# Block 0's transposes and the first two experts' sums of squares on TensorE, a routing step without GpSimd, and a new order of events

## The chip, the cores and the metric

One Trainium2 chip; the program runs on one of its cores. The metric is device time in microseconds (us) of one execution, lower is better. TensorE is PE in the rows, VectorE DVE, ScalarE ACT, GpSimd POOL; SP is the engine that issues the DMAs.

## The reference, cut to what matters

```python
x = attn(q, k, v, n_global=8, n_local=96)      # (2, 8, 768, 64): each row sees 8 global and 96 local keys
x = x.transpose(0, 2, 1, 3).reshape(1536, 512)
# MoE 1: dense, 4 experts
out = 0
for e in range(4):
    out += p[:, e:e + 1] * (np.maximum(x @ w1[e], 0) @ w2[e])     # w1[e] 512x1024, w2[e] 1024x512
x = out
# MoE 2: greedy, 8 experts with 192 places each
logits = x @ w_gate                            # (1536, 8)
# go through all (token, expert) pairs by falling logit; a pair is taken if its token
# has no expert yet and its expert has a free place
for e in range(8):
    mask = assigned == e
    out[mask] = np.maximum(x[mask] @ v1[e], 0) @ v2[e]
```

## The kernel before

All products run in fp16. A float32 operand is scaled by a power of two and split into a high and a low fp16 part (`hi`, `lo`), and three products of the parts are added. The power of two comes from a sum of squares: for a weight matrix ("job" k; jobs 0 to 7 are w1, w2 of the four experts of MoE 1, jobs 8 to 23 those of MoE 2) each half of 128x2048 is loaded by `w_load` (L397, 1 MB, issued on SP), squared on ACT with a running sum (`w_norm`, L437), the two sums go through a product with a matrix of ones (L441), `pow2` makes the scale on DVE (L316 to L321), and `w_split` makes the high parts on ACT (L548) and the low parts on DVE (L462), four pieces of 128x1024 each. A half's buffer is free for the next load when its second low part is done.

**First stage (to about 400 us).** Attention over 12 blocks of 128 tokens, interleaved with the products of experts 0 and 1 of MoE 1. Events of a block carry its number behind a dot (none for block 0): `load`, `loadv`; `sq0` to `sq2` (squares of v, k, q), `total`, `scale`; `hi0`, `lo0` and so on; `T0`, `T1` (transposes of q and k), `swap` (the two halves of q's heads exchanged); `qk0` to `qk3` (scores, L686 to L693), `max`, `exp` (L705, L707), `ph`, `pl` (high and low parts of the probabilities), `PT0`, `PT1` (their transposes), `pv` (L744), `x`, `norm`, `xhi`, `xlo`, `xT` (transpose of the attention's result). `g`, `relu`, `hhi`, `hlo`, `y` are the products of expert 0 (first product L825), `G`, `Relu`, `Hhi`, `Hlo`, `Y` those of expert 1; `wl`, `wsq`, `wsum`, `wsc`, `whi`, `wlo` prepare the weights. The transposes are DMAs (L633, L729, L761), and so are the two halves of `swap` (L626, L627). The order of the events is written out by hand in ORDER1, with the engine behind a slash where it isn't the usual one; every engine works its own part of it in that order.

**Second stage (to about 633 us).** Experts 2 and 3, the logits and their ranks; the events are sorted by times in a table (TIMES3). `pump` carries the preparation of the next weights on by one step.

**Routing (L1106 to L1199).** Seven iterations, each a chain on DVE with four short trips to PE: `best` (M, m, D), `pick` (a product and a sum, L1128 and L1130), `below` (v L1136, twelve products on PE L1141, a count L1144), `spread` (a product L1150), `pick`, `below`, `spread`, and the new `cut`. Behind each trip `between` puts some of the 93 deferred second products of expert 3 on PE (`fill`, L1003: two 512-column products each), steps of the finished token blocks (`side_step`: `add` L1013, `norm` L1019, and `rows_steps`, which scales a block, splits it into `hi` and `lo` and writes it to DRAM as rows, L1045 to L1058), and `pump`, as the list HOPS says.

**Last stage.** `gather` (L1207, on POOL's queue) fetches the rows of each expert of MoE 2 by the routing's indices, `gather_T` transposes them (L1216, on SP), and eight experts follow (first products L1238, second L1258). It can't start before the last block of rows has been written.

Of the kernel before, what the change touches and what calls it, by code (L numbers as in the profile page):

```python
# [45 lines left out]

ORDER1 = """
    load gate0 sq1 sq0 loadv wl0 gate1 slope4 gate2 sq2 total wl1 scale slope2 hi1 hi0/V lo0 diag/A slope3 wl0.1 wsq0
    load.1 wsq1 slope0 wsum wsq0.1 slope1 T0 lo1 wl1.1 T1 tiles.1 sq1.1 swap wsc slope5 whi1/G whi0/V wlo1 whi3 whi2
    wlo3 hi2/G lo2 qk0 sq0.1 wlo2 loadv.1 slope6 wlo0 wsq1.1 load.2 max0 sq2.1 wsum.1 wl0.2 wsc.1 qk1 whi1.1/G exp0  # L50
    total.1 slope7 scale.1 max1 hi1.1 hi0.1/V qk2 exp1 max2 qk3 lo0.1 exp2 whi2.1/G lo1.1 ph0/G wl1.2 T0.1 both
    whi3.1/V wsq0.2 sq1.2 pl0/G probs loadv.2 T1.1 wsq1.2 max3 ph2 wsum.2 whi0.1/V swap.1 ph1/G wlo1.1 exp3 pl1 sq0.2
    wlo0.1 diag.1/A wlo2.1 keys.1 ph3 wlo3.1 wsc.2 kglob.1 wl0.3 hi2.1 sq2.2 pl2/G qk0.1 total.2 pl3/G max0.1 wl1.3
    exp0.1 scale.2 qk1.1 PT0 hi1.2 tiles hi0.2/G max1.1 whi2.2/G lo0.2 exp1.1 qk2.1 ph0.1/G PT1 wsq0.3 lo2.1 qk3.1
    T0.2 max2.1 lo1.2 load.3 T1.2 consts diag.2 swap.2 pv keys.2 max3.1 x wsq1.3 norm ph1.1/A kglob.2 loadv.3 sq1.3
    values.1 exp2.1 pl0.1/G wsum.3 qk0.2 rscale xhi/G wsc.3 xlo exp3.1 xT pl1.1 vglob.1 gate3 ph2.1/A pl2.1 max0.2
    sq0.3 sq2.3 qk1.2 hi2.2/G total.3 g00 g01 scale.3 ph3.1/G hi1.3/V pe max1.2 exp0.2 pl3.1/G whi1.3 g02 hi0.3 g03
    lo1.3 qk2.2 whi0.2/G PT0.1 lo0.3 ph0.2 PT1.1 lo2.2 T0.3 g10 g11 pv.1 hi2.3 whi1.2 Both wlo2.2 g12 relu0 g13 max2.2
    exp1.2 T1.3 hhi0 x.1 pl0.2/G qk3.2 hlo0 norm.1 rscale.1 xhi.1/V y0 relu1 hhi1 exp2.2 load.4 xlo.1 max3.2 keys.3 y1
    sq1.4 y2 swap.3 exp3.2 hlo1 ph2.2/A ph1.2/G y3 y4 xT.1 diag.3 y5 kglob.3 pl1.2/G loadv.4 wlo1.2 y6 qk0.3 wlo0.2  # L60
    whi3.2 qk1.3 PT0.2 sq0.4 g00.1 max0.3 g01.1 g02.1 lo2.3 sq2.4 ph3.2 total.4 exp0.3 whi0.3 g03.1 pl2.2/G g10.1
    scale.4 qk2.3 max1.3 relu0.1/V y7 values.2/A g11.1 hi1.4/V g12.1 g13.1 pl3.2/G G00 lo1.4 G01 diag.4 max2.3 load.5
    ph0.3 vglob.2 exp1.3 hi0.4/G sq1.5 G02 relu1.1 hhi1.1 exp2.3 qk3.3 wlo3.2 PT1.2 ph1.3 hhi0.1 lo0.4 sq0.5 T1.4 pe.1
    ph2.3/A max3.3 loadv.5 G03 hlo0.1 hlo1.1 pv.2 exp3.3 y0.1 T0.4 G10 pl0.3 Tiles G11 y1.1 x.2 ph3.3 norm.2 pl1.3/G
    pl2.3/G sq2.5 pl3.3/G PT0.3 values.3/G swap.4 y2.1 y3.1 rscale.2 y4.1 keys.4/A y5.1 y6.1 whi3.3 whi2.3 total.5
    xhi.2/V kglob.4 hi2.4 PT1.3 Relu0 xlo.2 scale.5 Hhi0 qk0.4 qk1.4 hi1.5/G G12 G13 vglob.3 max0.4 hi0.5/G Relu1
    max1.4 pv.3 wlo3.3 x.3 y7.1 lo2.4 xT.2 Hhi1 g00.2 wlo0.3 norm.3 g01.2 load.6 g02.2 Hlo0/G g03.2 lo1.5 tiles.2
    exp0.4 g10.2 rscale.3 g11.2 Hlo1/G xhi.3/V xlo.3 qk2.4 g12.2 wlo1.3 sq1.6 loadv.6 relu0.2 exp1.4 max2.4 sq0.6
    lo0.5 add qk3.4 xT.3 g13.2 G00.1 wlo2.3 Pe hhi0.2 T0.5 Y0 G01.1 T1.5 sq2.6 total.6 hi2.5/V hlo0.2 Y1 ph0.4/G lo2.5
    pl0.4/G pe.2 scale.6 diag.5/A ph1.4/A add.1/V hi1.6/G Y2 Y3 relu1.2/V exp2.4 pl1.4/G hi0.6/V keys.5/G Y4 G02.1 Y5  # L70
    load.7 G03.1 Y6 ph2.4/A max3.4 exp3.4 Y7 kglob.5 sq1.7 pl2.4 y0.2 lo1.6 y1.2 swap.5 qk0.5 y2.2 sq0.7 ph3.4/A G10.1
    hhi1.2/V Tiles.1 PT0.4 y3.2 Relu0.1 pl3.4 G11.1 G12.1 hlo1.2/G max0.5 G13.1 g00.3 qk1.5 diag.6 hi2.6/V exp0.5 Pe.1
    qk2.5 loadv.7 g01.3 ph0.5/G y4.2 Hhi0.1 values.4/G lo0.6 sq2.7 max1.5 PT1.4 total.7 g02.3 Relu1.1/V Hhi1.1/G
    max2.5 g03.3 Hlo0.1 exp1.5 T1.6 qk3.5 exp2.5 vglob.4 scale.7 y5.2 pl0.5/G Hlo1.1 T0.6 y6.2 y7.2 pv.4 ph1.5/G Add
    Y0.1 hi1.7/V g10.3 max3.5 g11.3 swap.6 exp3.5 tiles.3 pl1.5 qk0.6 ph2.5/G hi0.7/V qk1.6 Y1.1 values.5 g12.3
    vglob.5 x.4 g13.3 max0.6 lo2.6 relu0.3 lo1.7 Y2.1 pl2.5 load.8 sq1.8 G00.2 hhi0.3 Y3.1 exp0.6 qk2.6 T1.7 max1.6
    lo0.7 hlo0.3/G loadv.8 Y4.1 G01.2 PT0.5 hi2.7/V relu1.3/V exp1.6 max2.6 norm.4 qk3.6 hhi1.3/V sq0.8 ph3.5/G T0.7
    rscale.4 sq2.8 G02.2 Y5.1 G03.2 hlo1.3/G pl3.5 PT1.5 diag.7/A max3.6 Y6.1 keys.7/A add.2/V xhi.4/V Relu0.2 total.8
    pe.3 G10.2 xlo.4 scale.8 lo2.7 hi1.8/V Y7.1 G11.2 exp2.6 Tiles.2 y0.3 hi0.8 y1.3 y2.3 y3.3 ph0.6/G y4.3 G12.2 y5.3
    pl0.6/G ph2.6/G Hhi0.2/V exp3.6 y6.3 lo1.8 pv.5 hi2.8/G xT.4 load.9 Add.1 Hlo0.2/G ph1.6/G swap.7 G13.2 loadv.9  # L80
    ph3.6/A lo2.8 x.5 pl2.6 pl1.6 Pe.2 Relu1.2 sq1.9 sq0.9 g00.4 sq2.9 y7.3 kglob.7 g01.4 qk0.7 g02.4 g03.4 total.9
# [1730 lines left out]
```

## Time and profile before

| | |
|---|---|
| time, median of 3 runs | 886.25 us (885.26 to 886.25) |
| profiled execution, its own time | 888.71 us |
| span of the profile | 886.9 us |
| mean granted TensorE clock | 0.971 |
| busy: PE, DVE, ACT, POOL | 775.8, 618.0, 500.4, 250.1 us |

The profiled execution lies 2.5 us above the median, and 1.8 us of it lie outside the span.

### The profile page before, as it was taken

The page shows a single profiled execution, that of the slowest core. Times are in us where ns is not written, and L with a number is a line of the kernel's source. Part 1 is how long each engine was busy: PE and PEld are TensorE (multiplying, and loading weights), DVE is VectorE, ACT ScalarE, POOL GpSimd, SP SyncE. Part 2 cuts the span into 40 slices and gives each one's busy share as a digit, 9 for nine tenths or more (in the row PEclk, how much of TensorE's full clock was granted, in tenths as well). Part 3 has the DMA queues.
Part 4 walks back from the last instruction along what each step waited for, and adds up shares of the span by engine and source line. Part 5 has one row for each costly group of instructions (what it writes and reads, how often), then busy time and mean ns, then how long its engine had stood idle before and what let it go on. Part 6 is the DMA issues. An engine that isn't in the chain of part 4 may idle for free. (4 is left out here: it accounts for less than half of the span.)

```text
span 886.9 us, 20995 instructions
## 1 busy us (share of the span) xinstructions
PE 775.8 (87%) x8540; PEld 594.9 (67%) x8545; DVE 618.0 (70%) x1557; ACT 500.4 (56%) x978; POOL 250.1 (28%) x299
## 2 busy tenths in 40 slices
...
GB/s 238 273 201 167 135 161 158 143 149 101 81 71 181 49 49 49 160 127 26 13 14 24 2 26 24 26 96 2 167 72 72 73 233 320 225 256 337 177 37 38
DMA packets 196865, 105.31 MB, mean 119 GB/s; under 512 B 167584, under 2 KB 167584, under 8 KB 196768
## 3 DMA queue, kind: packets, MB, share of 16 engines
...
q0 software_dynamic: 2048, 6.34, 3.0%
...
## 5 line engine op out<-in xcount | busy, mean ns | idle before, releaser
L825 PEld LDWEIGHTS <-w 128*128 128x128 f16 x3456 | 246.4, 98 | 31.2 <-issue 0.6
L825 PE MATMUL pH<-xT,w 128*128 128x128 f16 (+1 forms) x3168 | 246.9, 234 | 0.4 <-ACT H L799 0.4
L836 PE MATMUL pY<-w,hh 128*128 128x512 f16 x544 | 161.8, 379 | 0.0
L836 PE MATMUL pY<-w,hl 128*128 128x512 f16 x272 | 103.1, 379 | 1.6 <-DVE hl L1385 1.6
L971 ACT ACTIVATE Cj<-C 128x128 bf16<-128x128 bf16 (+11 forms) x88 | 75.3, 855 | 42.4 <-DVE C L958 41.5
L1238 PEld LDWEIGHTS <-w 128*128 128x128 f16 x768 | 67.4, 102 | 23.0 <-DMA xg<-g 17.2
L799 ACT ACTIVATE H<-pH 128x512 f32<-128x512 f32 (+1 forms) x83 | 46.1, 561 | 60.0 <-PE pH L825 48.5
L958 DVE TENSOR_SCALAR C<-w,Lg 128x1024 bf16<-128x1024 f32 (+7 forms) x112 | 72.6, 665 | 3.8 <-PE pw L977 1.8
L836 PEld LDWEIGHTS <-hh 128*128 128x128 f16 x544 | 47.3, 98 | 34.5
L1238 PE MATMUL pH<-xg,w 128*128 128x192 f16 x528 | 51.7, 258 | 17.8 <-DMA xg<-g 16.7
L1258 PE MATMUL pR<-hh,w 128*128 128x192 f16 x512 | 67.0, 249 | 0.0
L1258 PEld LDWEIGHTS <-w 128*128 128x128 f16 x768 | 65.3, 100 | 0.3
L1258 PE MATMUL pR<-hl,w 128*128 128x192 f16 x256 | 63.9, 250 | 0.0
L1003 PE MATMUL pY<-w,xT 128*128 128x512 f16 x192 | 62.4, 400 | 0.0
L707 ACT ACTIVATE t<-pS,mx,ec 128x256 f32<-128x256 f32 (+1 forms) x96 | 51.6, 541 | 2.7 <-issue 0.4
L550 POOL TENSOR_SCALAR hh<-H 128x512 f16<-128x512 f32 x38 | 26.4, 696 | 89.2 <-ACT H L799 57.6
L836 PEld LDWEIGHTS <-hl 128*128 128x128 f16 x272 | 26.6, 98 | 34.9 <-DVE hl L1385 3.3
L722 POOL TENSOR_TENSOR pp<-t,pp 128x512 f16<-128x512 f32 (+1 forms) x27 | 35.3, 1306 | 41.1 <-DVE pp L552 20.6
L462 DVE SCALAR_TENSOR_TENSOR w<-raw,wsr,w 128x1024 f16<-128x1024 f32 x32 | 40.3, 1278 | 9.0 <-ACT w L548 8.8
L1003 PE MATMUL pY<-w,hl 128*128 128x512 f16 x112 | 45.5, 406 | 0.0
L552 DVE TENSOR_SCALAR hh<-H 128x384 f16<-128x384 f32 (+1 forms) x48 | 18.7, 389 | 38.3 <-ACT H L799 38.2
L961 DVE SCALAR_TENSOR_TENSOR jk<-w,Lg,notbefore 128x128 bf16<-128x128 f32 x96 | 42.6, 444 | 0.0
...
## 6 DMA issues: line engine op xcount, KB each, us to landing
w<-in_moe_w_dram SPq DMA_DIRECT2D x16, 1024.0 KB, 7.0
raw<-in_moe_w_dram SPq DMA_DIRECT2D x16, 1024.0 KB, 7.9
hl<-in_moe_w_dram SPq DMA_DIRECT2D x8, 1024.0 KB, 5.5
y<-in_moe_w_dram SPq DMA_DIRECT2D x4, 1024.0 KB, 8.0
xT<-in_moe_w_dram SPq DMA_DIRECT2D x4, 1024.0 KB, 8.1
rows<-xs SPq DMA_DIRECT2D x12, 260.0 KB, 2.0
...
```

The source lines that it names most:

```text
L462: V.scalar_tensor_tensor(l, r[:, d2], sc, h, op0=OP.mult, op1=OP.subtract)
L707: s.nc.scalar.activation(t[:, hh], ps[:, hh], AF.Exp, bias=mx[:, 1, hh:hh + 1], scale=e[:, 0:1], accum_out=s.SU[j][:, 2 * g + hh:2 * g + h ...
L722: (G if eng == "G" else V).tensor_sub(pl[:, x], t, ph[:, x])
L799: s.nc.scalar.activation(H, ps, AF.Relu, scale=HS)
L825: nc.tensor.matmul(o[f], w[:, d, 128 * (f0 + f):128 * (f0 + f) + 128], x[:, :, c], start=(d == 0 and i == 0), stop=(d == 3 and i == 2))
L836: nc.tensor.matmul(py, l[:, f], w[:, f], start=(f == 0 and i == 0), stop=(f == 7 and i == 2))
L958: V.tensor_scalar(C[:, 8 * i:8 * i + n], x[:, :n, e], l, None, op0=OP.is_ge)
L961: V.scalar_tensor_tensor(jk, s.LRof[j][:, e], l, s.notbefore, op0=OP.is_equal, op1=OP.mult, accum_out=s.AC[j][:, 0, e:e + 1])
L971: s.nc.scalar.activation(x, C, AF.Copy, accum_out=s.AC[j][:, 1, e:e + 1])
L1003: nc.tensor.matmul(py, a[:, f], w[:, f], start=(n == 0), stop=(n == 23))
L1238: nc.tensor.matmul(ps[0][:, f % 2], w[:, d, 128 * f:128 * f + 128], xg[:, :, c], start=(k == 0), stop=(k == 11))
L1258: nc.tensor.matmul(ps[0][:, d % 2], w[:, f, 128 * d:128 * d + 128], h[:, f], start=(k == 0), stop=(k == 23))
```

## The change

1. **Block 0's transposes.** With TURNED = 1 the `T0`, `T1`, `swap`, `PT0`, `PT1` and `xT` of block 0 are products with an fp16 identity matrix on TensorE (`turn`), four at a time into a PSUM tile that ACT or DVE copies out. The other blocks keep their DMA transposes.
2. **Squares by TensorE.** With BYPE = 4 the sums of squares of jobs 0 to 3 are 32 products each of the weights' upper bf16 halves with themselves, whose diagonal DVE adds up.
3. **Sums in bf16.** The sums of squares are held in bf16, so the product with ones is a bf16 one.
4. **ORDER1** is written anew, with some events on other engines.
5. **Second stage:** pumps become events of the same table; the list ORDER3 is empty, so events are sorted by the same times.
6. **`rows_steps`** is now one ACT operation for `hi`, a DVE one for `lo`, and a small ACT operation for the scale; POOL keeps a memset.
7. **`route`** takes the rank from the minimum by two shifts, instead of a `pick`.
8. **`between`** calls `pump` once each, and the weights' preparation stops ahead of the splits of jobs 8 and 9 until the 29th call (`s.limit`).

```diff
     def w_norm(s, k, q):
+        if k < BYPE and q < 2:
+            if q == 0:
+                J["gram"] = s.pY.tile([128, 512], F32, name="pY")[:, 0:128]
+            x = s.raws[k, q][0].bitcast(BF)
+            for a in range(4):
+                for b in range(4):
+                    y = x[:, a, 256 * b + 1:256 * b + 256:2]
+                    nc.tensor.matmul(J["gram"], y, y, start=(q + a + b == 0), stop=(q == 1 and a + b == 6))
+            return
+        if k < BYPE and q == 2:
+            jk = s.sm.tile([128, 128], BF, name="gramj", bufs=1)
+            V.scalar_tensor_tensor(jk, J.pop("gram"), 1.0, s.ident, op0=OP.mult, op1=OP.mult, accum_out=J["ss"][:, 0:1])
+            J["ps"] = s.pw[:, k:k + 1]
+            nc.tensor.matmul(J["ps"], s.ones, J["ss"][:, 0:1], start=False, stop=True, skip_group_check=True)
+            return
...
+    def turn(s, o, parts):
+        nc = s.nc
+        for a in range(0, o.shape[1], 4):
+            ps = s.pH.tile([128, 4, 128], F32, name="pH")
+            for i in range(4):
+                n = 0
+                for x in parts(a + i):
+                    m = x.shape[1]
+                    nc.tensor.matmul(ps[n:n + m, i], x, s.identh, start=True, stop=True)
+                    n += m
+            if a % 8:
+                nc.vector.tensor_copy(o[:, a:a + 4], ps)
+            else:
+                nc.scalar.activation(o[:, a:a + 4], ps, AF.Copy)
...
     def rows_steps(s, j, sc, inv):
-            if late:
-                s.scaled_on("V" if j == s.NB - 1 else "A", xs[:, 0:512], x, sc)
-            else:
-                nc.scalar.activation(x, x, AF.Copy, scale=sc)
-                nc.scalar.copy(xs[:, 0:512], x)
-            nc.gpsimd.tensor_scalar(xs[:, 1024:1026].bitcast(F32), inv, 1.0 / HS, 0.0, op0=OP.mult, op1=OP.add)
+            s.scaled_on("V" if j == s.NB - 1 else "A", xs[:, 0:512], x, sc)
+            nc.scalar.activation(xs[:, 1024:1026].bitcast(F32), inv, AF.Copy, scale=1.0 / HS)
             nc.gpsimd.memset(xs[:, 1026:], 0.0)
...
-            if late:
-                nc.vector.scalar_tensor_tensor(xs[:, 512:1024], x, sc, xs[:, 0:512], op0=OP.mult, op1=OP.subtract)
-            else:
-                nc.gpsimd.tensor_sub(xs[:, 512:1024], x, xs[:, 0:512])
+            nc.vector.scalar_tensor_tensor(xs[:, 512:1024], x, sc, xs[:, 0:512], op0=OP.mult, op1=OP.subtract)
...
         for it in range(E - 1):
-            D = best()
-            r = pick(D, s.R, "r")
+            D, m = best()
+
+            r = rk.tile([128, NB], I32, name="r")
+            V.tensor_scalar(r, m, 21, 21, op0=OP.logical_shift_left, op1=OP.logical_shift_right)
...
-            s.loadlimit, s.limit = 16, 10
+            s.loadlimit, s.limit = 16, 8
...
             def between():
-                fill(HOPS[2 * s.nfill])
+                fill(HOPS[s.nfill])
                 s.nfill += 1
...
-                s.pump(HOPS[2 * s.nfill - 1])
+                s.pump(1)
+                if s.nfill > 28:
+
+                    s.limit = 10
+                    s.pump(3)
```

On SP's queue at the start of the program, before (the transposes are L633 of block 0, the swap is L626 and L627; y and xT hold the halves of job 0 and 1, and xT again of job 2):

```order
5 L475 DMA y<-in_moe_w_dram 128x4x512 x2
6 L475 DMA xT<-in_moe_w_dram 128x4x512
7 L560 DMA x<-in_k_dram 128x8x64
8 L560 DMA x<-in_q_dram 128x8x64
9 L633 DMA_TRANSPOSE qT<-qn 128x8x128
10 L475 DMA xT<-in_moe_w_dram 128x4x512
11 L633 DMA_TRANSPOSE kT<-kn 128x8x128
12 L626 DMA qT<-qT 64x1024
13 L627 DMA qT<-qT 64x1024
```

The same place of the changed kernel:

```order
5 L494 DMA y<-in_moe_w_dram 128x4x512 x2
6 L494 DMA xT<-in_moe_w_dram 128x4x512 x2
7 L579 DMA x<-in_k_dram 128x8x64
8 L579 DMA x<-in_q_dram 128x8x64
9 L579 DMA x<-in_v_dram 128x8x64
10 L579 DMA x<-in_k_dram 128x8x64
11 L579 DMA x<-in_q_dram 128x8x64
12 L494 DMA y<-in_moe_w_dram 128x4x512 x2
13 L675 DMA_TRANSPOSE qT<-qn 128x8x128
```

Block 0's four DMAs are gone from between the loads; block 1's q transpose is the first one left.

On DVE in the second iteration of the routing, before (L1128 and L1130 with R are the `pick` of the rank, L462 a low part of job 8):

```order
1092 L1120 TENSOR_REDUCE m<-M 128x12
1093 L1122 TENSOR_TENSOR D<-M,m 128x96
1094 L1128 TENSOR_TENSOR pt<-D,R 128x96
1095 L1130 TENSOR_REDUCE r<-pt 128x12
1096 L1136 TENSOR_TENSOR v<-r,t_9917 128x480
1097 L462 SCALAR_TENSOR_TENSOR w<-w_9913,wsr,w 128x2x512
1098 L1144 TENSOR_SCALAR vt,kk<-pq 8x40
1099 L1013 SCALAR_TENSOR_TENSOR y<-pY,pe_5_6348,y 128x512
```

The corresponding piece of the changed kernel, in its fifth iteration:

```order
1111 L1158 TENSOR_REDUCE m<-M 128x12
1112 L1160 TENSOR_TENSOR D<-M,m 128x96
1113 L1195 TENSOR_SCALAR r<-m 128x12
1114 L1174 TENSOR_TENSOR v<-r,t_10115 128x480
1115 L1182 TENSOR_SCALAR vt,kk<-pq 8x40
1116 L1059 SCALAR_TENSOR_TENSOR y<-pY,pe_8_6553,y 128x512
```

One shift stands for two operations, and no low part of the weights lies between v and its count.

On ACT behind the routing, before (sqj is `norm` of block 10 and 11, xs the `hi` of block 10; the splits of raw and w_9913 are job 10's; junk is the square of a later job):

```order
407 L1019 ACTIVATE sqj,rq_10731<-y 128x512
408 L548 ACTIVATE w<-w_9914,wsr 128x1024
409 L548 ACTIVATE xs<-y,rgr 128x512
410 L1019 ACTIVATE sqj,rq_10775<-y 128x512
411 L548 ACTIVATE w_10812<-raw,wsr 128x2x512 x2
412 L548 ACTIVATE w_10812<-w_9913,wsr 128x2x512 x2
413 L437 ACTIVATE junk,wss<-raw 128x2048
```

The same place of the changed kernel (row 415 writes the scale of block 11 into its rows, w_10111 is the buffer that held job 8's halves and is loaded again with the second half of job 10 for row 413 and the first of job 11 for row 417; w_10112 is job 9's):

```order
407 L1065 ACTIVATE sqj,rq_10871<-y 128x512
408 L456 ACTIVATE y,wss<-raw 128x2048
409 L567 ACTIVATE w<-w_10111,wsr 128x2x512 x2
410 L567 ACTIVATE xs<-y,rgr 128x512
411 L1088 ACTIVATE xs<-rgr 128x1
412 L1065 ACTIVATE sqj,rq_10923<-y 128x512
413 L456 ACTIVATE y,wss<-w_10111 128x2048
414 L567 ACTIVATE w<-w_10111,wsr 128x2x512
415 L1088 ACTIVATE xs<-rgr 128x1
416 L567 ACTIVATE w<-w_10112,wsr 128x1024 x2
417 L456 ACTIVATE y,wss<-w_10111 128x2048
```

Squares of jobs 10 and 11 and the last high part of job 8 now stand ahead of row 415, which belongs to the last block of rows.

On DVE at the same place of the changed kernel (rows 1177 and 1179 are `hi` and `lo` of block 11, rows 1168, 1178 and 1180 low parts of jobs 8 and 9):

```order
1167 L1059 SCALAR_TENSOR_TENSOR y<-pY,pe_11_6559,y 128x512
1168 L481 SCALAR_TENSOR_TENSOR w<-w_10111,wsr,w 128x2x512
1169 L1093 SCALAR_TENSOR_TENSOR xs<-y,rgr,xs 128x512
...
1177 L571 TENSOR_SCALAR xs<-y,rgr 128x512
1178 L481 SCALAR_TENSOR_TENSOR w<-w_10111,wsr,w 128x2x512
1179 L1093 SCALAR_TENSOR_TENSOR xs<-y,rgr,xs 128x512
1180 L481 SCALAR_TENSOR_TENSOR w<-w_10112,wsr,w 128x1024 x3
```

The last low part of job 8 stands between `hi` and `lo` of block 11; before, the two were neighbours.

On SP around the last rows, of the changed kernel (before, both loads of w_9913 stood ahead of the last six row writes):

```order
151 L400 DMA raw<-in_moe_w_dram 128x4x512
152 L1096 DMA rows<-xs 128x1040 x9
153 L400 DMA w_10111<-in_moe_w_dram 128x4x512
154 L1096 DMA rows<-xs 128x1040 x2
155 L400 DMA w_10111<-in_moe_w_dram 128x4x512
156 L1096 DMA rows<-xs 128x1040
157 L1256 DMA_TRANSPOSE xg<-g 128x8x96 x4
```

The second of those loads now stands directly ahead of the write of block 11.

## Rows read from the trace of the kernel before

**Rows 1.** Busy time by stretch, windows view: length, each engine's busy us, granted clock, DMA share.

```profile
core 0: us, PE busy (x) PEld busy (x) DVE busy (x) ACT busy (x) POOL busy (x), PEclk, DMA share, GB/s
...
30.00:40.00 10.00, 2.65 (x16) 1.89 (x13) 9.96 (x20) 8.54 (x22) 4.73 (x7) 1.00 0.96 258
...
100.00:150.00 50.00, 48.13 (x644) 37.27 (x643) 44.82 (x101) 32.89 (x95) 21.77 (x20) 1.00 0.75 137
...
633.00:700.00 67.00, 56.99 (x385) 25.07 (x383) 53.63 (x164) 35.77 (x52) 14.17 (x27) 0.90 0.28 99
```

**Rows 2.** PE's timeline, first 64 us: start, duration, operation, idle before and what ended it.

```profile
26.01 0.27 PE L692 MATMUL pS<-kT,qT 128*128 128x128 f16 x1 [6.61 <-DMA kT<-kn]
...
42.53 0.31 PE L692 MATMUL pS<-kT,qT 128*128 128x128 f16 x1
42.63 0.31 PE L693 MATMUL pS<-kT,qT 128*128 128x128 f16 x1
...
52.40 1.70 PE L744 MATMUL pO<-vs,pt 128*128 128x64 f16 x24 [3.40 <-DMA pt<-pp]
...
63.09 1.07 PE L825 MATMUL pH<-xT,w 128*128 128x128 f16 x10
```

**Rows 3.** ACT's groups by line in the first 64 us: busy, mean ns of one, idle before.

```profile
L437 ACT ACTIVATE w<-y 128x2048 f16<-128x2048 f32 x4 | 7.6, 1906 | 2.3 <-DMA y<-in_moe_w_dram 2.3
```

**Rows 4.** DMA issues in the first 64 us: KB each, median us from issue to landing.

```profile
pt<-pp SPq DMA_TRANSPOSE x4, 3.9
...
kT<-kn SPq DMA_TRANSPOSE x3, 4.3
```

**Rows 5.** DVE's timeline in the routing: end of iteration 5, iteration 6, and a disturbed v.

```profile
674.42 0.14 DVE L1168 TENSOR_TENSOR cut<-cut,pq 128x8 f32<-128x8 f32 x1
...
675.77 0.26 DVE L1128 TENSOR_TENSOR pt<-D,R 128x96 f32<-128x96 bf16 x1
...
676.35 0.66 DVE L1136 TENSOR_TENSOR v<-r,t 128x480 bf16<-128x480 f32 x1
...
682.19 0.16 DVE L1168 TENSOR_TENSOR cut<-cut,pq 128x8 f32<-128x8 f32 x1 [0.31 <-PE pq L1150]
...
688.36 1.62 DVE L1136 TENSOR_TENSOR v<-r,k 128x480 bf16<-128x480 f32 x1
```

**Rows 6.** POOL's timeline beside that v.

```profile
688.31 1.15 POOL L1055 TENSOR_TENSOR xs<-y,xs 128x512 f16<-128x512 f32 x1
```

**Rows 7.** DVE's groups by line, 633 to 700 us.

```profile
L462 DVE SCALAR_TENSOR_TENSOR w<-w,wsr,w 128x1024 f16<-128x1024 f32 x7 | 8.9, 1273 | 0.0
```

**Rows 8.** DVE's timeline from the end of the routing to the last rows.

```profile
700.06 0.74 DVE L1013 SCALAR_TENSOR_TENSOR y<-pY,pe,y 128x512 f32<-128x512 f32 x1
...
707.01 0.75 DVE L1053 SCALAR_TENSOR_TENSOR xs<-y,rgr,xs 128x512 f16<-128x512 f32 x1
...
710.07 2.48 DVE L462 SCALAR_TENSOR_TENSOR w<-w,wsr,w 128x1024 f16<-128x1024 f32 x2
```

**Rows 9.** ACT's timeline at the same place, up to the first square behind it.

```profile
707.81 2.17 ACT L548 ACTIVATE w<-w,wsr 128x1024 f16<-128x1024 f32 x2
726.33 1.91 ACT L437 ACTIVATE junk<-raw 128x2048 f16<-128x2048 f32 x1 [16.34 <-DMA raw<-in_moe_w_dram]
```

**Rows 10.** POOL's timeline: the first four gathers.

```profile
710.72 1.64 POOL L1207 DMA_INDIRECT g<-rows,idx  x1 [4.14 <-DMA rows<-xs]
712.66 0.93 POOL L1207 DMA_INDIRECT g<-rows,idx  x1 [0.30 <-issue]
```

**Rows 11.** PE's timeline: the first product of the last stage.

```profile
719.78 2.58 PE L1238 MATMUL pH<-xg,w 128*128 128x192 f16 x15 [16.71 <-DMA xg<-g]
```

**Rows 12.** DMA issues, 655 to 664 us, as in rows 4.

```profile
w<-in_moe_w_dram SPq DMA_DIRECT2D x1, 1024.0 KB, 5.1
rows<-xs SPq DMA_DIRECT2D x1, 260.0 KB, 2.0
```

**Rows 13.** DMA issues, 700 to 735 us, as in rows 4.

```profile
raw<-in_moe_w_dram SPq DMA_DIRECT2D x5, 1024.0 KB, 10.1
```

More of the change, by code (lines that the diff above doesn't have):

```diff
@@ L45 @@
 LAG = 2
+BYPE, TURNED = 4, 1
 ORDER1 = """
[L48 to L71, printed above, removed]
@@ L77 @@
[L77 to L81, printed above, removed]
@@ new lines @@
+    norm wsq0.3 max2.1 max3.1 wsq1.3 pl0.1/G exp2.1 consts pl1.1/G tiles.1 rscale wsum.3 exp3.1 keys.2/G xhi/V xlo
+    load.3 kglob.2 swap.2 ph2.1/A pl2.1/G ph3.1 xT loadv.3 PT0.1 diag.2/A pl3.1/G sq1.3 wsc.3 PT1.1 g00 gate3 qk0.2
+    values.1/G sq0.3 max0.2 sq2.3 qk1.2 total.3 scale.3 Both g01 pe exp0.2 hi1.3 g02 hi0.3/G ph0.2/A g03 qk2.2 max1.2
+    whi0.2/G lo0.3 g10 lo1.3 exp1.2 relu0/V T0.3 vglob.1 pv.1 hhi0 x.1 whi1.2 hi2.2/G max2.2 g11 hlo0/G norm.1 lo2.2
+    rscale.1 g12 g13 y0 y1 xhi.1/V hi2.3 T1.3 load.4 y2 qk3.2 diag.3 ph1.2/G swap.3 relu1 xlo.1 hhi1 y3 whi2.2 hlo1
```

213 lines of the change are left out of this document (131 added, 82 removed).

## The prediction

> **What bounds the kernel now.** I read the windows view first, then PE's timeline at the start, the groups of ACT and the DMA issues there, then DVE's, ACT's and POOL's timelines from the routing to the last stage. Three places have PE waiting, and the change touches all three.
>
> The start: in 30 to 40 us PE is busy 2.65 of 10 us, while DVE has 9.96 [rows 1]. The first scores wait 6.61 us for a DMA transpose and start at 26.01, block 0's `pv` waits 3.40 us for another at 52.40, and the first expert product starts at 63.09 [rows 2]. Behind it PE is nearly full, 48.13 of 50 us in 100 to 150 [rows 1]: whatever comes before 63 us shifts what follows by as much, as long as PE's later work is the same. ACT meanwhile squares 128x2048 weights at 1.91 us each and waits for the loads [rows 3].
>
> The routing: in 633 to 700 us PE is busy 56.99 of 67.0 us at a granted clock of 0.90, DVE 53.63 us [rows 1]. Neither is full: the chain goes back and forth between them. Iteration 6 runs from 674.42 to 682.19, 7.77 us [rows 5].
>
> The last rows: the one-hot matrix of the routing is done at 700.06, call this T. The `lo` of block 11 starts at 707.01 and ends at T+7.7 [rows 8]; its rows, at 2.0 us a write [rows 12], have landed by T+9.7. The first gather starts at 710.72 [rows 10] and the first product at 719.78, T+19.7 [rows 11]. Behind the high parts that end at 709.98, ACT has nothing to do until 726.33, for 16.34 us [rows 9].
>
> **The change, part by part.**
>
> Start. It removes the DMA transposes of block 0 and its swap; a DMA transpose takes 3.9 to 4.3 us from issue to landing [rows 4]. In their place come 8 products each for `T0`, `T1`, `PT0`, `PT1` and `xT` and 16 for `swap`, 56 in all. Two 128-column products start 0.10 us apart [rows 2], so these are 5.6 us of PE. The copies out, 12 of 128x512, I price by the 0.74 us of a DVE operation of that size that reads PSUM [rows 8]: 8.9 us, half of it on ACT and half on DVE. The squares of jobs 0 to 3 were eight at 1.91 [rows 3], 15 us of ACT; they become 128 products, at 0.10 us 13 us of PE. All this PE time lies in a stretch where PE idles 7 us in 10 [rows 1]. ACT comes out some 11 us lighter (15 less 4.4). ORDER1 also moves operations off DVE; I count the loss of copies and the moves as about even, with DVE some us lighter at best. The bf16 product with ones replaces an fp32 one off the bound, worth nothing that I can see.
>
> What does it save? The two waits that the DMA transposes caused, 6.61 + 3.40 = 10.0 us [rows 2]. The products that take their place run in the remaining gaps. From below: if only the second wait disappears on the path, 3.4. From above: if half of ACT's relief reaches the path as well, 10.0 + 5.5, say 16. I take **10**, since the first wait is where block 0 begins, and ACT's relief pays for the copies. The first expert product should then stand near 53 us.
>
> PE works in program order, so the sums of squares can also hold back: the products for job 0 wait for the second half of its load, with block 0's `swap` queued behind them, and behind those the scores. That load lands early enough (ACT squares both halves before PE's first scores), so I take nothing; if job 1's loads come late, the 3.4 holds.
>
> Second stage: same order by the same table; nothing.
>
> Routing. The pick of the rank costs 676.35 - 675.77 = 0.58 us an iteration [rows 5]; a shift replaces it, at about 0.2 (an estimate from the smallest DVE operations here, 0.14 and 0.16 [rows 5], on a few more elements). Seven times 0.38 is 2.7 us of DVE. The seven low parts inside, 8.9 us [rows 7], move behind T. The `lo` of nine blocks goes from POOL to DVE, about nine at 0.75 [rows 8], plus 6.8 us, and takes away disturbances: v took 1.62 us instead of 0.66 where POOL's subtraction ran beside it [rows 5, 6], 0.96 us. How many of the nine subtractions cost that I leave at four, 3.8 us. DVE: -2.7 - 8.9 - 3.8 + 6.8 = -8.6 of its 53.63. PE keeps the same deferred products, so the routing can't fall below PE's busy 57.0 unless the clock rises: 67.0 - 57.0 = 10.0 us is the most at the clock of before. At full clock it would be 0.90 x 57.0 = 51.3, 15.7 less. From below: 3, if the trips to PE wait behind the deferred products as they do now and only the pick is saved. I take **10**; with fewer DVE operations between trips PE is the one that sets the pace.
>
> Behind the routing. What left the routing stands ahead of block 11's rows. By the order: DVE's `add` of block 10 (0.74 [rows 8]), ACT's `norm` of the same size (0.7, estimated from it), ACT's square of the first half of job 10 (1.9), a high part (2.17 / 2 = 1.1 [rows 9]), the second low part of job 8 (2.48 / 2 = 1.24 [rows 8]): T+5.7. Only then is the buffer free, and SP issues the load of job 10's second half: 5.1 us when alone [rows 12], T+10.8. ACT's square of it stands in front of the fourth high part of job 8, and that in front of the last low part, which stands between `hi` and `lo` of block 11: 1.9 + 1.1 + 1.24 + 0.75 = 5.0, T+15.8. Queued behind that waiting square on ACT are also block 11's scale and job 9's high parts. On SP the load of job 11's first half goes out just before the write of block 11 (its buffer comes free at T+15.0), so the write lands somewhere between 2.0 us after its issue, T+17.8, and behind the load and its own bytes, 15.0 + 5.1 + 1, T+21.1. I take 20.5. Before it was T+9.7, so the loss is 8.1 to 11.4, and I take **10.8**.
>
> The gathers then run beside low parts of jobs 9 and 10 on DVE. Before, the first gather took 1.64 us beside two low parts [rows 8, 10], the second 0.93 alone: 0.71 us each. Of the other three one more may meet such an operation: **0.7**, with bounds of 0 and 2.1. On this the Trainium skill (page “SBUF — State Buffer”, section “SBUF: two separate sides”) says that VectorE and GpSimd share a port pair under an exclusive lock, and that a DMA issued from GpSimd can't have its descriptors written while VectorE holds it. By that rule all of the gathers could be held, and the sum would be 1.4 us higher; the trace agrees in the one gather that ran beside such work.
>
> Block 11's delay is not paid twice: job 9's and job 10's splits, about 15 us of ACT, now fill the 16.34 us in which ACT waited [rows 9], and the last stage's order is as before.
>
> **Sum.** -10 - 10 + 10.8 + 0.7 = -8.5 us. The span of 886.9 becomes 878.4. The profiled execution's own time, 888.71, lies 2.5 above the median of 886.25; I take the difference from the median: **877.8 us**.
>
> **The rivals.**
>
> A. The routing goes further. With GpSimd silent and DVE lighter the gaps close so well that the granted clock, 0.90 over the routing [rows 1], stays up. Then the routing gives 15, and the front and tail lie at the better halves of their bounds (12 and 9): 886.25 - 12 - 15 + 9 = 868. For it: the clock was lost after PE's waits. Against it: waits between trips remain.
>
> B. The start gives little. Block 1 keeps its DMA transposes and comes right behind; DVE was busy 9.96 of 10 us in 30 to 40 [rows 1], and the copies add to it. Then the start gives 3.4 or less: 886.25 - 3 - 10 + 11.5 = 884.8.
>
> C. Slower: the late load. Both loads behind T are priced at 5.1; in 700 to 735 loads took 10.1 [rows 13]. There several stood in the queue, here they are alone but for rows. If each takes L, the loss grows by 2 (L - 5.1), once through ACT's square and once through the write queued behind the other. It cancels the sum of 8.5 at L = 9.35; at 10.1 the time is 877.8 + 10.0 = 887.8. For it: it is the only place with a load's whole latency on the path. Against it: alone, the load took 5.1.
>
> D. The change doesn't do what it says in the routing: the trips keep waiting behind deferred products, PE's 57 us stretch as before, and 3 us are saved: 886.25 - 10 - 3 + 11.5 = 884.8.
>
> **Chances.** Forecast (870 to 882) 0.52, A 0.16, B 0.12, C 0.12, D 0.08. About 0.2% either side, 1.8 us, is what a measurement of this kernel can tell from no change: 884.5 to 888.0. The forecast and A lie below; of B and D, at its edge, I put half below, and half of the rest inside; C lies half inside, half above. Faster 0.78, same 0.11, slower 0.11. The range of 865 to 886 leaves out C and the far end of A.
>
> **What would show it.** First expert product near 53 us, first scores near 20, no wait of PE for kT or pt of block 0. From the start of the routing to its one-hot matrix about 57 us, PE nearly without gaps, v at 0.66 everywhere. ACT waiting for a weights' load just behind T, the last rows written near T+16 and landed near T+20, the first product of the last stage at T+30. Wrong would be: block 1 waiting where block 0 did, with the first expert product past 60; the last rows landed before T+12 or after T+25; or a stall in the first stage's later blocks, where the new order was taken to be as good as the old.

## The result and the profile after

The changed kernel takes 872.9 us (median, 867.5 to 874.0) against 885.8 of the kernel before: a ratio of 0.985 (0.980 to 0.990). The forecast was 877.8 us, in a range of 865 to 886. Run again beside other kernels it took 871.6 us, 0.986 (0.982 to 0.989). The profiled execution has a span of 870.1 us, 16.8 shorter than before; its own time is 871.9.

PE's timeline of the changed kernel, at the same places as in [rows 2] and [rows 11], with some rows ahead of them (L446 are the products for job 0's sum, L651 block 0's transposes, L734 and L735 the scores, L789 `pv`, L873 the first expert product, L1278 the first product of the last stage):

```profile
10.49 1.89 PE L446 MATMUL pY<-y 128*128 128x128 bf16 x16 [3.04 <-DMA y<-in_moe_w_dram]
12.18 1.05 PE L651 MATMUL pH<-identh,qn 128*128 128x128 f16 x8
...
17.26 0.22 PE L734 MATMUL pS<-kT,qT 128*128 128x128 f16 x1
...
17.72 0.22 PE L734 MATMUL pS<-kT,qT 128*128 128x128 f16 x1
17.78 0.22 PE L735 MATMUL pS<-kT,qT 128*128 128x128 f16 x1
...
25.16 0.31 PE L734 MATMUL pS<-kT,qT 128*128 128x128 f16 x1
25.27 0.31 PE L735 MATMUL pS<-kT,qT 128*128 128x128 f16 x1
...
39.92 1.06 PE L789 MATMUL pO<-vs,pt 128*128 128x64 f16 x14
41.15 0.68 PE L789 MATMUL pO<-vs,pt 128*128 128x64 f16 x10 [0.18 <-DVE pt L654]
...
48.72 1.53 PE L873 MATMUL pH<-xT,w 128*128 128x128 f16 x12 [0.58 <-ACT xT L656]
...
707.04 1.30 PE L1278 MATMUL pH<-xg,w 128*128 128x192 f16 x7 [18.73 <-DMA xg<-g]
```

The two waits of 6.61 and 3.40 us for DMA transposes are gone; the first expert product comes 14.4 us earlier than in [rows 2]. The routing starts at 617.54 instead of 632.92, 15.4 us earlier: the gain at the start is carried through the 570 us between, in which PE is nearly full. DVE's timeline, the begin and end of the routing and the rows of block 11 (L1059 is `add`, L1093 the low part of the rows, L481 low parts of job 8):

```profile
617.54 0.25 DVE L1147 SCALAR_TENSOR_TENSOR Z<-Q,R 128x96 f32<-128x96 f32 x1
...
673.37 1.36 DVE L1232 TENSOR_TENSOR Coh<-cc,c 128x1152 f16<-128x1152 f32 x1
674.64 0.74 DVE L1059 SCALAR_TENSOR_TENSOR y<-pY,pe,y 128x512 f32<-128x512 f32 x1
...
689.16 1.28 DVE L481 SCALAR_TENSOR_TENSOR w<-w,wsr,w 128x1024 f16<-128x1024 f32 x1 [4.21 <-ACT w L567]
690.37 0.75 DVE L1093 SCALAR_TENSOR_TENSOR xs<-y,rgr,xs 128x512 f16<-128x512 f32 x1
```

From the routing's start to T it is 57.1 us, where it was 67.1; T is 674.6. The windows view of that stretch, columns as in [rows 1]: PE is busy 51.4 instead of 57 us, at a granted clock of 0.97 instead of 0.90, DVE 41.7 instead of 53.6.

```profile
617.50:674.60 57.10, 51.42 (x375) 22.61 (x373) 41.73 (x152) 19.64 (x39) 1.03 (x10) 0.97 0.22 81
```

From T to the first product of the last stage it is 32.4 us, where it was 19.7. ACT's timeline there shows the square that waits for the load, and what it holds up:

```profile
686.09 1.91 ACT L456 ACTIVATE y<-w 128x2048 f16<-128x2048 f32 x1 [3.67 <-DMA w<-in_moe_w_dram]
...
688.00 1.13 ACT L567 ACTIVATE w<-w,wsr 128x1024 f16<-128x1024 f32 x1
689.03 0.19 ACT L1088 ACTIVATE xs<-rgr 128x1 f32<-128x1 f32 x1
```

SP's timeline: the load of job 11's first half, and 0.8 us later the write of block 11's rows.

```profile
690.47 0.38 SPq L400 DMA_DIRECT2D w<-in_moe_w_dram  x1
691.26 0.32 SPq L1096 DMA_DIRECT2D rows<-xs  x1
701.42 5.91 SPq L1256 DMA_TRANSPOSE xg<-g  x4
```

The DMA issues from 689 to 700 us: the write took 5.9 us to land, as long as the load ahead of it; it took 2.0 before [rows 12].

```profile
w<-in_moe_w_dram SPq DMA_DIRECT2D x1, 1024.0 KB, 6.0
rows<-xs SPq DMA_DIRECT2D x1, 260.0 KB, 5.9
```

In sum: start and what it carries -15.4, routing -10.0, T to the last stage +12.7, and the last stage itself, 163.1 us instead of 167.1, -4.1. That is the span's -16.8; the medians differ by 12.8, since the profiled execution of the kernel before took 888.7 us, 3 more than its median, and that of the changed kernel 1 less.

### The profile page after: what moved, and what is told of

Same layout as the page of the kernel before. It is cut to its first block, busy times and chain, and to the rows that moved or that the text cites. A ratio compares the mean times of both kernels' runs of the same rounds, so it can differ in the third digit from the quotient of the medians.

```text
span 870.1 us, 21221 instructions
## 1 busy us (share of the span) xinstructions
PE 769.3 (88%) x8660; PEld 591.3 (68%) x8664; DVE 612.3 (70%) x1545; ACT 494.4 (57%) x989; POOL 244.7 (28%) x287
## 5 line engine op out<-in xcount | busy, mean ns | idle before, releaser
L873 PEld LDWEIGHTS <-w 128*128 128x128 f16 x3456 | 246.5, 98 | 37.4 <-issue 5.4
L873 PE MATMUL pH<-xT,w 128*128 128x128 f16 (+1 forms) x3168 | 249.1, 234 | 3.7 <-ACT H L847 2.7
L1017 ACT ACTIVATE Cj<-C 128x128 bf16<-128x128 bf16 (+11 forms) x88 | 75.3, 855 | 42.5 <-DVE C L1004 41.6
L1278 PEld LDWEIGHTS <-w 128*128 128x128 f16 x768 | 66.7, 102 | 37.0 <-DMA xg<-g 23.4
L1278 PE MATMUL pH<-xg,w 128*128 128x192 f16 x528 | 51.8, 259 | 22.0 <-DMA xg<-g 19.5
L1298 PE MATMUL pR<-hh,w 128*128 128x192 f16 x512 | 64.9, 246 | 0.0
L1049 PE MATMUL pY<-w,xT 128*128 128x512 f16 x192 | 60.4, 389 | 0.0
L569 POOL TENSOR_SCALAR hh<-H 128x512 f16<-128x512 f32 x40 | 28.5, 713 | 101.2 <-ACT H L847 76.0
L764 POOL TENSOR_TENSOR pp<-t,pp 128x512 f16<-128x512 f32 (+1 forms) x34 | 39.8, 1175 | 44.4 <-ACT pp L567 36.0
L481 DVE SCALAR_TENSOR_TENSOR w<-w,wsr,w 128x1024 f16<-128x1024 f32 x32 | 40.3, 1279 | 13.4 <-ACT w L567 13.4
L1425 POOL TENSOR_TENSOR hl<-H,hh 128x512 f16<-128x512 f32 x26 | 32.9, 1267 | 56.4 <-DVE hh L571 31.7
L481 DVE SCALAR_TENSOR_TENSOR w<-raw,wsr,w 128x1024 f16<-128x1024 f32 x32 | 40.2, 1279 | 7.5 <-ACT w L567 7.2
```

The costliest lines, as they stand in the source:

```text
L481: V.scalar_tensor_tensor(l, r[:, d2], sc, h, op0=OP.mult, op1=OP.subtract)
L764: (G if eng == "G" else V).tensor_sub(pl[:, x], t, ph[:, x])
L873: nc.tensor.matmul(o[f], w[:, d, 128 * (f0 + f):128 * (f0 + f) + 128], x[:, :, c], start=(d == 0 and i == 0), stop=(d == 3 and i == 2))
L1017: s.nc.scalar.activation(x, C, AF.Copy, accum_out=s.AC[j][:, 1, e:e + 1])
L1049: nc.tensor.matmul(py, a[:, f], w[:, f], start=(n == 0), stop=(n == 23))
L1278: nc.tensor.matmul(ps[0][:, f % 2], w[:, d, 128 * f:128 * f + 128], xg[:, :, c], start=(k == 0), stop=(k == 11))
```

## The experiments

Each was timed beside the kernel before on its chip, and the ratios are to that. The stamps of all profiles, in us (FE first expert product, R routing's start, T one-hot matrix done, L first product of the last stage):

| kernel | FE | R | R to T | T to L | end | time | ratio |
|---|---|---|---|---|---|---|---|
| before | 63.1 | 632.9 | 67.1 | 19.7 | 886.9 | 885.8 | 1 |
| changed | 48.7 | 617.5 | 57.1 | 32.4 | 870.1 | 872.9 | 0.985 (0.980 to 0.990) |
| changed, again (e11) | 49.2 | 617.2 | 54.8 | 31.8 | 870.2 | 871.6 | 0.986 (0.982 to 0.989) |
| e1 DMA transposes back | 62.3 | 633.0 | 55.5 | 32.4 | 884.0 | 887.0 | 0.999 (0.996 to 1.003) |
| e2 squares back on ACT | 60.7 | 633.6 | 54.8 | 31.7 | 882.3 | 884.9 | 0.998 (0.995 to 1.001) |
| e3 both back, new order | 66.8 | 638.9 | 55.2 | 32.8 | 890.3 | 897.0 | 1.013 (1.008 to 1.018) |
| e4 splits in the routing | 51.0 | 619.5 | 64.3 | 20.0 | 868.8 | 866.7 | 0.977 (0.972 to 0.982) |
| e5 load behind the rows | 48.6 | 617.2 | 55.0 | 28.9 | 864.9 | 869.7 | 0.984 (0.977 to 0.990) |
| e6 rows first | 50.5 | 620.4 | 54.9 | 31.8 | 877.1 | 881.8 | 0.998 (0.994 to 1.001) |
| e7 rows first, job 8 first | 49.0 | 619.1 | 57.9 | 24.8 | 864.4 | 864.2 | 0.975 (0.969 to 0.981) |
| e8 pick back | 49.6 | 617.8 | 56.2 | 32.0 | 871.4 | 873.8 | 0.988 (0.981 to 0.995) |
| e9 loads behind transposes | 50.6 | 619.4 | 55.1 | 29.2 | 867.0 | 871.2 | 0.987 (0.982 to 0.991) |
| e10 low parts on POOL | 50.0 | 619.4 | 57.5 | 32.1 | 873.4 | 874.6 | 0.989 (0.985 to 0.992) |
| e12 no early sums | 50.2 | 620.1 | 55.1 | 20.4 | 864.4 | 865.5 | 0.973 (0.970 to 0.976) |

The stamps are of one execution each, the times are medians. The profiled executions lay up to 4.9 us from their medians: that of e3 took 892.1 us and was the shortest of its five, that of e4 took 870.6 and was the longest.

**The start: e1, e2, e3.**

```diff
-BYPE, TURNED = 4, 1
+BYPE, TURNED = 4, 0      # e1: DMA transposes for block 0
+BYPE, TURNED = 0, 1      # e2: squares of jobs 0 to 3 on ACT
+BYPE, TURNED = 0, 0      # e3: both, only the order is new
```

> The changed kernel with block 0's transposes as DMAs again, all else as changed (first expert product at 48.7 us, 872.9 us in all). Theory, that the DMA transposes' waits held the start: the first expert product goes back by about 10 us, to 58 to 60, and the time to 882 to 884. Rival, that the order and the lighter ACT gave the start its gain: the first expert product stays ahead of 53, the time below 877.

> The changed kernel with the sums of squares of jobs 0 to 3 on ACT again, transposes of block 0 still on TensorE. Theory: ACT was 8.0 to 9.2 us of 10 busy from 20 to 50 us in the changed kernel, so 15 us of squares put back reach the path in part: first expert product 52 to 55, time 876 to 879. Rival, that the products for the sums hold block 0 back on TensorE as much as ACT's squares would: first expert product at 47 to 50, time within 2 us of 872.9.

> The changed kernel with both put back: DMA transposes and squares on ACT, only the new order of events stays. Theory: first expert product at 62 to 66 as before the change, time 885 to 889. Rival, that the order itself is the gain: first expert product ahead of 55, time below 880.

With DMA transposes the first expert product goes back by 13.6 us to 62.3, more than expected, and so does the time, 887.0. PE's timeline of e1 has waits for DMA transposes again, for the swapped `qT`, for `pt` and for `xT`:

```profile
22.31 0.27 PE L735 MATMUL pS<-kT,qT 128*128 128x128 f16 x1 [5.26 <-DMA qT<-qT]
...
49.18 0.82 PE L789 MATMUL pO<-vs,pt 128*128 128x64 f16 x12 [4.04 <-DMA pt<-pp]
...
62.29 1.44 PE L873 MATMUL pH<-xT,w 128*128 128x128 f16 x12 [5.68 <-DMA xT<-xs]
```

The squares on ACT cost nearly as much, 12.0 us, where I expected 3 to 6. The windows view of e2 shows why: ACT is nearly full from 20 to 50 us, and PE, at 1.6 to 6.0 of 10, waits for it; behind it PE's timeline has the longest of these waits.

```profile
20.00:30.00 10.00, 2.02 (x20) 1.34 (x17) 6.85 (x11) 9.93 (x21) 4.47 (x5) 1.00 0.66 175
30.00:40.00 10.00, 1.63 (x14) 1.34 (x14) 8.43 (x17) 9.90 (x21) 4.91 (x5) 1.00 0.63 171
40.00:50.00 10.00, 5.96 (x65) 4.64 (x64) 7.47 (x20) 9.46 (x24) 4.61 (x6) 1.00 0.93 261
```

```profile
39.87 0.16 PE L460 MATMUL pq<-wss,ones 128*128 128x1 bf16 x1 [7.10 <-ACT w L456]
```

The new order alone starts the first expert product at 66.8, 3.7 later than before, and at 897.0 it is slower than expected; that it is laid for the other two parts is the likely cause. From there the transposes alone gain 6.1 us (e2), the products for the squares alone 4.5 (e1), both together 18.1. By these stamps two limits stand side by side, and taking away one leaves much of the other. The medians don't say so: from e3's 897.0 the transposes gain 12.1, the products 10.0, both 24.1, nearly the sum. e3's profile is 4.9 us under its median, and where its other executions lose more is not on record; whether the two gains add or not stays open. By both readings the rivals by which one of the two, or the order, was the whole gain are out. In all runs R moves with FE: R less FE is 568 to 573 us in every row. The bf16 sums and the second stage's new table have no run of their own.

**The routing: e4, e8, e10.** e4 lets the splits of jobs 8 and 9 back in:

```diff
-            s.loadlimit, s.limit = 16, 8
+            s.loadlimit, s.limit = 16, 10
```

> The changed kernel with the splits of jobs 8 and 9 allowed inside the routing again. Theory: the eight low parts, 1.28 us each, lie partly on the chain again, routing 57.1 to about 63 us, but nothing waits for a load behind it, so the distance from the one-hot matrix to the first product of the last stage goes from 32.4 back to about 20: time 865 to 868. Rival one, that TensorE's deferred products set the routing's pace alone: routing stays at 57 to 58, time near 860. Rival two, that the routing gained only by these splits leaving: routing back to 66 or 67, time 869 to 871.

The routing takes 64.3 us, T to L is 20.0. So the splits are worth 7.2 us of the routing's 10.0 (up to 9.5, by the other runs of 54.8), and sending them behind T cost 12.4: this part of the change was a net loss, and e4 is the faster kernel, at a ratio of 0.977 against 0.985 and 0.986, with intervals that just touch. The time is as expected. The windows view of e4's routing has DVE 10 us busier than in the changed kernel, PE 2 us; PE is idle for 10.9 us of it, where it is 5.7 in the changed kernel:

```profile
619.50:683.80 64.30, 53.44 (x379) 23.39 (x377) 51.69 (x168) 32.14 (x54) 1.03 (x10) 0.95 0.30 104
```

e8 takes the rank by a product and a sum again:

```diff
-            r = rk.tile([128, NB], I32, name="r")
-            V.tensor_scalar(r, m, 21, 21, op0=OP.logical_shift_left, op1=OP.logical_shift_right)
+            r = pick(D, s.R, "r")
```

> The changed kernel with the rank taken by a product and a sum again instead of by the shift, seven times 0.38 us more on DVE. Theory by the sum: up to 2.7 us, routing at 59 to 60, time 875 to 876. Rival, that TensorE's deferred products set the pace: routing at 57 to 57.5, time within 1 us of 872.9.

Routing 56.2 us, between the changed kernel's two profiles, 57.1 and 54.8. These two differ in the granted clock, 0.97 and 1.00, and in PE's busy time, 51.4 and 50.0. e8's clock is 1.00, so it belongs beside e11 and beside e1 to e3, which have 1.00 and the same routing, 54.8 to 55.5: the shift is worth 0.7 to 1.4 us, not 2.7. The time, 873.8, is within 1 us of 872.9, as the rival has it. The windows views of e8, with DVE 2.7 us busier, and of e11:

```profile
617.80:674.00 56.20, 50.02 (x375) 22.34 (x373) 44.43 (x159) 19.54 (x39) 1.03 (x10) 1.00 0.23 83
```

```profile
617.20:672.00 54.80, 49.97 (x375) 22.31 (x373) 41.66 (x153) 19.64 (x39) 1.03 (x10) 1.00 0.23 85
```

e10 puts the low parts of nine blocks on POOL again, with their two ACT operations for `hi` (cut here):

```diff
...
-            nc.vector.scalar_tensor_tensor(xs[:, 512:1024], x, sc, xs[:, 0:512], op0=OP.mult, op1=OP.subtract)
+            if j > 8:
+                nc.vector.scalar_tensor_tensor(xs[:, 512:1024], x, sc, xs[:, 0:512], op0=OP.mult, op1=OP.subtract)
+            else:
+                nc.gpsimd.tensor_sub(xs[:, 512:1024], x, xs[:, 0:512])
```

> The changed kernel (872.9 us) with the low parts of the first nine blocks of rows on POOL again and their two ACT operations, the splits still out of the routing. Theory: POOL's subtractions stretch DVE's operations beside them, about 0.96 us each where they meet one, while DVE is spared 0.75 each: routing at 57 to 60, time 873 to 876. Rival, that the disturbances were the larger part of what the routing lost before: routing at 62 or more, time 878 or more.

Routing 57.5 us, against 54.8 and 57.1. Its clock is 0.97, as in the profile of 57.1, so the low parts' move is worth about 0.4 us, and 2.7 at most. The windows view:

```profile
619.40:676.90 57.50, 51.63 (x375) 22.55 (x373) 39.23 (x143) 24.68 (x49) 11.70 (x20) 0.97 0.22 81
```

DVE's timeline of e10 still has stretched operations, but only two longer than 0.9 us inside the iterations (0.26 us each elsewhere), where the kernel before had v at 1.62 [rows 5]:

```profile
620.60 1.04 DVE L1167 TENSOR_TENSOR D<-Z,m 128x96 bf16<-128x96 f32 x1
...
670.64 0.96 DVE L1162 TENSOR_TENSOR M<-R,cut 128x96 f32<-128x96 f32 x1
```

**Behind the routing: e5, e6, e7, e9, e12.** e5 moves one load behind the last write:

```diff
-            s.loadlimit, s.limit = 16, 8
+            s.loadlimit, s.limit = 11, 8
...
+            s.loadlimit = 16
             W = s.finish(2, 0)
```

> The changed kernel (872.9 us) with one load moved: the first half of job 11 is issued on SP behind the write of block 11's rows instead of just ahead of it. There the write was issued 16.6 us after the one-hot matrix (T) and the first gather began at T+23.5, 6.9 us after the issue against 2.0 us for a write alone. Theory, that the write stood behind the load: the first gather begins at T+18.5 to T+20, the first product of the last stage at T+28 instead of T+32.4, time 868 to 869.5. Rival, that the write is slow for another cause, or that the later load is paid at job 11: the first gather at T+23 or the time unchanged within 1.5 us.

The first gather begins at 691.86, T+19.6 (T+23.5 in the changed kernel), and T to L is 28.9, 3.5 us less. The write, now issued ahead of that load, lands in 2.1 us instead of 5.9, so it did stand behind the load. The time, 869.7, is in the expected direction, but its interval overlaps that of the changed kernel; the stamps decide this, not the time. The DMA issues of e5 from 688 to 692 us, POOL's timeline of e5, and behind it that of the changed kernel (the row of e5 names a low part on DVE as what ended the wait, not the write, which had landed 1 us earlier):

```profile
rows<-xs SPq DMA_DIRECT2D x1, 260.0 KB, 2.1
```

```profile
691.86 1.33 POOL L1247 DMA_INDIRECT g<-rows,idx  x1 [20.11 <-DVE w L481]
```

```profile
698.15 1.13 POOL L1247 DMA_INDIRECT g<-rows,idx  x1 [24.25 <-DMA rows<-xs]
699.59 0.93 POOL L1247 DMA_INDIRECT g<-rows,idx  x1 [0.30 <-issue]
700.82 0.92 POOL L1247 DMA_INDIRECT g<-rows,idx  x1 [0.30 <-issue]
702.04 1.27 POOL L1247 DMA_INDIRECT g<-rows,idx  x1 [0.30 <-issue]
```

e6 and e7 keep the splits behind the last rows; e7 also has job 9's squares in the routing and all of job 8's parts ahead of any square that waits for a load.

```diff
                 s.pump(1)
-                if s.nfill > 28:
-                    s.limit = 10
-                    s.pump(3)
+                if s.nfill in (27, 28):              # e7 alone
+                    s.w_norm(9, s.nfill - 27)
+                    s.nst[9] = s.nfill - 26
             s.route(between)
             while fills:
                 fill(3)
-                s.pump(1)
             while s.side:
                 s.side_step()
-                s.pump(1)
+            s.limit, s.early = 10, (0, 0, 0, 0)      # e6: only s.limit = 10
             W = s.finish(2, 0)
```

> The changed kernel with the splits of jobs 8 and 9 kept behind the last rows altogether, in the order that the planner then gives (job 9's and job 10's squares still come between job 8's parts). Theory: routing stays at 57, the last rows are issued about 6.5 us after the one-hot matrix, the first product of the last stage starts at T+18 to T+20 instead of T+32.4, but job 8's last parts wait for a load and squares until T+26, so that 4 to 6 of the 13 us are lost again: time 863 to 867. Rival, that the weights are then late throughout (ACT and the loads bound the last stage): time 870 or more.

> As the run before, with job 9's two squares inside the routing and all eight parts of job 8, then job 9's, right behind the last rows, ahead of any square that waits for a load. Theory: first product at T+18 to T+20 and no wait behind it until job 10: time 858 to 863, faster than with splits in the routing (866.7). Rival, that the loads of the last stage set its end: it starts 12 us earlier and ends less than 5 us earlier, 868 or more.

e6 missed, at 881.8. The rows were out early (the first gather ran at 684.9, T+9.6), but L stayed at T+31.8. SP's timeline shows why, which neither theory had: the second of two loads waits 9.3 us on SP for its buffer, and the transposes of the gathered rows stand behind it. That alone would leave e6 level with the changed kernel. It is slower by its last stage, 170.0 us instead of 163.1, which fits the rival: weights that are late throughout, and a time of 870 or more.

```profile
689.82 10.15 SPq L400 DMA_DIRECT2D w<-in_moe_w_dram  x2
700.08 6.93 SPq L1256 DMA_TRANSPOSE xg<-g  x4
```

In e7 the buffers come free early, these loads are issued within 2.8 us, and L is T+24.8: later than the T+18 to T+20 expected, but at 864.2, just above the 858 to 863 expected, the time is faster than that of the changed kernel. e9 moves those loads behind the transposes:

```diff
-            s.limit, s.early = 10, (0, 0, 0, 0)
+            s.limit, s.early, s.loadlimit = 10, (0, 0, 0, 0), 10
...
-            s.pump(WAITS[2])
...
-            s.pump(WAITS[3])
+            s.pump(WAITS[2] + WAITS[3])
```

> The rows-first kernel with squares ahead (864.2 us, first product of the last stage 24.8 us after the one-hot matrix) with its two loads behind the last rows moved on behind the transposes of the gathered rows, and the planner's steps there with them. Theory, that those loads hold the gathers and transposes back: first product at T+18 to T+20. What it is worth then is open: if the loads are free to come later, time 859 to 862; rival, that the squares of the late loads hold ACT and the last stage ends by its loads: time 864 to 870 in spite of the earlier first product.

The transposes are now issued by T+20.7, yet L is T+29.2, and the time rises to 871.2: both theories missed. PE's timeline of e9: a product for job 10's sum, ahead of the first product in PE's queue, waits 9.29 us for ACT's square of a late load.

```profile
694.24 0.16 PE L460 MATMUL pw<-wss,ones 128*128 128x1 bf16 x1 [14.98 <-ACT junk L456]
703.69 0.16 PE L460 MATMUL pw<-wss,ones 128*128 128x1 bf16 x1 [9.29 <-ACT junk L456]
703.72 6.96 PE L1278 MATMUL pH<-xg,w 128*128 128x192 f16 x48
```

e12 takes those steps out:

```diff
-            s.pump(WAITS[2] + WAITS[3])
+            s.w_load()
```

> The run before the last (loads behind the transposes, 871.2 us) with the planner's nine steps ahead of expert 0's first products taken out: there TensorE's sum for job 10, which waits for ACT's square of a late load until 703.7, stood in its queue ahead of the first product, though the transposes had been issued by 695.2. Theory: the first product starts at T+20 to T+21 instead of T+29, and the time falls to 862 to 866. Rival, that expert 1's weights are then the next thing late (their second half lands 25 us or more behind T, and ACT's squares of it stand ahead of expert 0's hidden values): the start moves by 8 us, the time by less than 4, to 867 to 871.

L is T+20.4, as expected; PE's timeline of e12 has only the transposes left to wait for:

```profile
695.64 5.94 PE L1278 MATMUL pH<-xg,w 128*128 128x192 f16 x48 [15.75 <-DMA xg<-g]
...
711.51 0.16 PE L460 MATMUL pw<-wss,ones 128*128 128x1 bf16 x1 [4.99 <-ACT junk L456]
```

L moved by 8.8 us and the time by 5.7 (by 2.6 in the two profiles): from L to the end it takes 168.8 us instead of 163.3, and the sums for the next weights now hold PE there. The time, 865.5, is in the theory's range; that the next weights are late, as the rival has it, holds too. At 0.973 of the kernel before, e12 is with e7 and e4 (0.975, 0.977) the fastest; their intervals overlap, so which of the three is best stays open.

e11 is the changed kernel once more:

> The changed kernel unaltered, beside the runs before on one chip. Both theories: 870 to 875, ratio to the kernel before 0.983 to 0.987; its spread is what the other runs of this kind are read against.

It gave 871.6 us at 0.986.

## Why the prediction came out as it did

The time was in the range, and the three large terms came out with the signs forecast, 4.9 us lower in sum. In the profiles the gap is larger, -16.8 against the -8.5 forecast: 5.4 of it from the start, 4.1 from the last stage, and 1.2 the other way behind the routing.

**Start: right in its mechanism, too small.** Forecast -10, measured -14.4. The two waits of 10.0 us are gone, as told. The mis-sized step is "ACT's relief pays for the copies": I let ACT's squares count for nothing beyond that, but e2 shows ACT as the other limit, 12.0 us by itself when the squares come back. The upper bound of 16 had half of that relief in it, and the truth lay nearer to that end. "I take nothing" for PE's order was wrong too: `qn` of block 0 was done at 9.6 us, but its transposes started at 12.18, behind the products for job 0, which had waited 3.04 us for a load. What these 2.6 us cost no run shows; the scores still came at 17.26, ahead of the 20 forecast. Rival B is out: block 1's DMA transposes did not become the next limit. That a shift at 63 us reaches the routing held in every run to within 4 us.

**Routing: right in sum, wrong in parts.** Forecast -10, measured -10.0, and 12 in several other runs. I let PE's 10.0 us of idle time vanish at the clock of before. By the windows views its idle time fell only to 5.7, and its busy time from 57.0 to 51.4, as the granted clock rose from 0.90 to 0.97: that the sum agrees is luck. I gave the pick 2.7 us, and it is worth 0.7 to 1.4 (e8); POOL's silence 3.8 less 6.8 for DVE's extra work, a loss of 3.0, and it is a gain of about 0.4 (e10); the splits' leaving, 8.9, made 7.2 to 9.5 of the gain (e4). The step that failed is the adding of DVE's operations: with the splits gone PE is busy for nine tenths of the routing, and an operation less on DVE is worth little of its length. That this is because PE sets the pace fits e8 and e10, but no run takes work from PE. The bound "the routing can't fall below PE's busy 57.0 unless the clock rises" held in its second half. Rival A's mechanism was thus half there; D is out.

**Behind the routing: right.** Forecast +10.8 and +0.7, measured +12.7. The chain is as told: ACT waited 3.67 us for the load, the scale of block 11 was held behind it, and `lo` of block 11 ended at T+16.5 (T+15.8 forecast). The two loads took 5.7 us (from 680.4 to ACT's start at 686.1) and 6.0, not 5.1, so the write landed at T+22.5, not T+20.5. Rival C was wrong by the size of L: at 5.7 and 6.0 it costs 1.5 us. The +0.7 for the gathers did not come: the last three ran beside low parts on DVE, which go on from 699.60 to 707.48 with short gaps, and took 0.93, 0.92 and 1.27 us, where those that ran alone before took 0.93 [rows 10]; the first took 1.13 with DVE idle. The four sum to less than before. My 0.71 compared a first gather with a second: against a first one alone, 1.13, the 1.64 of before is 0.51 more. The rule of the Trainium skill that I cited there (page “SBUF — State Buffer”, section “SBUF: two separate sides”) was stretched: for the descriptors of such a DMA the section names VectorE operations in a 2-port mode, and two SBUF inputs, as the low parts have, it counts only against a GpSimd operation that reads SBUF. These gathers hardly bear my reading out: beside this kind of low part one of three took 0.34 longer, the others nothing.

**Not forecast: the last stage.** It took 163.1 us instead of 167.1. In the changed kernel's second profile it took 166.4, in e1 to e3, whose code there is the same, 162.3 to 163.4. Of the kernel before there is one profile. A term that I put at nothing may be in it: "The bf16 product with ones replaces an fp32 one off the bound". In the last stage these products took 8.1 us of PE before and 3.2 behind the change, half as many and 165 ns each instead of 245. PE's groups from L to the end, before and after (idle time behind the second bar):

```profile
L441 PE MATMUL pw<-wss,onesf 128*128 128x1 f32 x52 | 8.1, 245 | 8.1 <-ACT junk L437 8.1
```

```profile
L460 PE MATMUL pw<-wss,ones 128*128 128x1 bf16 x26 | 3.2, 165 | 7.8 <-ACT junk L456 7.8
```

No run puts the fp32 sums back alone. Whether the change shortens this stage, and by what, stays open.
